# Where a mixture-of-experts kernel issues the casts and subtractions of its second weights, and its gate's steps

## The chip, the cores and the metric

The kernel runs on one core of a Trainium2 chip. The metric is device time in microseconds (us) of one launch. An engine name in a row is the profile's: PE is TensorE's matmul, PEld its weight load, DVE is VectorE, ACT is ScalarE, POOL is GpSimd, and SP issues the DMAs.

## What is computed

The reference is three stages on 1536 tokens of width 512:

```python
x = attention(q, k, v)          # 2 x 8 heads x 768 x 64, 4 sink columns and a window of 128
P = exp(x @ w_gate - max)       # 1536 x 8
for _ in range(8):              # rows, then columns
    P /= P.sum(1, keepdims=True) + 1e-9
    P /= P.sum(0, keepdims=True) + 1e-9
    P *= N / E
for e in range(8):              # every token goes through every expert
    out += P[:, e:e+1] * (relu(x @ w1[e]) @ w2[e])      # 512 -> 1024 -> 512
g = out @ w_in;  g -= tanh(g)                           # 512 -> 2048
return g @ w_out                                        # 2048 -> 512
```

## The kernel before

All products are made of pairs: an operand is split into a high part (`fp32r`, by a cast on ACT) and a low part (the operand less its high part, by a subtraction on DVE or POOL), and three products of parts are summed in PSUM.

**The mixture** (`mixture`, L772) works in 32 half experts, `for u in range(units)` (L859): 16 for the first 768 tokens, 16 for the others. Half expert `u` holds 512 of the 1024 hidden columns in two quartets, a and b, and goes through the list `order` (L856). A step such as `5b` is one of the seven products of a Strassen-like scheme (`product`, L818: six matmuls of 384 columns) for quartet b. Products 1, 6 and 7 write one PSUM bank and their sums are copied out by ACT (`kept`, L812, names `p1`, `u2`, `u3`); products 2, 3 and 7 add such a copy by DVE (`plus`, L816); `put` (L803) then makes the hidden tile by a relu on ACT (L805) and its low part on DVE (L806). Product 6 accumulates on the bank that product 1 left, and 7 on what 6 left, so each waits for the ACT copy before it. The steps g0 to g2, G0 to G2 and A3 to A5 are the second products (`second`, L741: matmuls of 512 columns): g and G take quartets a and b of token tiles 0 to 2, A both of tiles 3 to 5. After G and A, DVE adds the PSUM bank to the sum over experts (L940 in half expert 1, L942, L947), which frees one of the three banks of `ps_g`.

**Weights.** `stage1_next` and `stage2_next` load raw first and second weights by SP's queue. `sum_next` (L549) makes four sums of one raw first tile on POOL (L553); `split1_next` and `split2_next` cast on ACT (L588) and subtract (L591). Of the four casts of first weights per half expert, issued from g2 to G2, three are subtracted on DVE; the fourth is kept in `deferred` and is subtracted on POOL, issued at the start of the next half expert (L868). One second weight is cast and subtracted (on POOL) at that start as well (L870), the other behind product 1a (L901), and there both calls of `sum_next` follow. Every subtraction issues the next load behind it on SP's queue. Each engine works its queue in order, so an instruction issued at a start of a half expert can run earlier on an engine that is ahead of PE.

**Narrow steps.** Up to half expert 28, `some_narrow` (L888) puts ten DVE instructions into each half expert (L686 to L701, eight per piece of 128x512, none in half experts 0, 1 and 15): they round the last layer's weights, one behind 5b, one behind 3a, and one behind each of g0, g1, G0, G1, G2, A3, A4 and A5.

**The gate** (`gates`, L706) is a generator of eleven steps, one taken at each place named in `gate_steps` (L858): the largest logit, its transpose, its broadcast with the first row sums, then eight times a matmul by ones (`pc`, L730) followed by nine DVE instructions (L731 to L735, then L724 to L727) whose result the next `pc` needs. The logits of the second half of the tokens are made in half expert 0 (`gate_logits`, behind 1b to 3a).

**The last layer** (`last_layer`, L976) runs 16 steps of four units (`g1_unit`, `g2_unit`). The first 768 tokens of its input are transposed (`x2_tile`, L969) in half expert 31.

Of the kernel before, what the change touches and what calls it, by code (L numbers as in the profile page):

```python
# [7 lines left out]
F32 = mybir.dt.float32  # L8
# [9 lines left out]
P = 128  # L18
# [5 lines left out]
KD = DM // P  # L24
# [17 lines left out]
class Kernel:  # L42
# [729 lines left out]
    def mixture(self, ctx, gp):  # L772
# [20 lines left out]
        for s in (4, 5, 6):  # L793
            fill(0, s)()
        w2_steps = [step() for _ in range(2) for step in self.split2_next()]
        self.gate_done = False
# [60 lines left out]
        pending, deferred = [], []  # L857
        gate_steps = {0: "g2 G0 G1 A3 A4 A5", 1: "6a 2b 3a g1 G1 A3 A4"}  # L858
        for u in range(units):  # L859
# [6 lines left out]
            held = {}  # L866

            if deferred:  # L868
                deferred.pop()(G)
            if u:  # L870
                w2_steps = [step() for step in self.split2_next()]
            for step in w2_steps:
                step(G)
            if u == 2:
                for i in range(NI):
                    V.tensor_scalar(
                        out=self.acc(0, i), in0=self.acc(0, i), scalar1=prob[:, i, 0:1], scalar2=None, op0=ALU.mult
                    )
            if u == 8:
                for i in range(4):  # L880
                    for k in range(2):
                        self.t_sum(1, i, k, G)
            todo, logits = [], list(range(NI, 2 * NI)) if u == 0 else []
# [10 lines left out]

            for step in order:
                kind, n = step[0], step[1]
                if kind in "1234567":
                    product(qa if n == "a" else qb, int(kind))
                    if logits and step in ("1b", "7a", "2b", "4a", "5b", "3a"):
                        self.gate_logits(logits.pop(0), ps_g, "g")  # L900
                    if step == "1a":  # L901
                        if u:
                            for x in self.split2_next():
                                x()(G)
                        if u < units - 1:
                            self.sum_next()
                            self.sum_next()
                    if step in gate_steps.get(u, "").split():
                        self.gate_bank = lambda shape, name: ps_g.tile(shape, F32, tag="g", name=self.nm(name))
                        next(gates, None)  # L910
                    if step in ("5b", "3a"):
                        some_narrow(1)
                    continue
# [8 lines left out]
                if step == "g2":  # L922
                    todo = self.split1_next() + self.split1_next()
                    if u == units - 1:
                        todo += self.split1_next()
                if todo:
# [23 lines left out]
                if x2s and kind != "g":  # L950
                    self.x2_tile(0, x2s.pop(0), ps_g)
            for second in pending:
# [15 lines left out]

    def x2_tile(self, b, n, pool):  # L969
        pt = pool.tile([P, KD, P], F32, tag="g", name=self.nm("x2"))  # L970
        for d in range(KD):
# [4 lines left out]
    def last_layer(self, ctx, gp):  # L976
# [71 lines left out]

        for _ in range(2):
            for step in self.split2_next():  # L1050
                step()(G)
        for s in range(steps + 1):
            for f in range(4):
                if s < steps:
                    g1_unit(s, f)
                    if (s % 4, f) in ((1, 0), (3, 2)) and s > 1:
                        for step in self.split1_next():
                            step()(G)
                    if (s % 4, f) in ((1, 2), (2, 2)):
                        for step in self.split2_next():  # L1060
                            step()(G)
                elif f == 0:
                    finish_units()
# [39 lines left out]
```

## Time and profile before

| | |
|---|---|
| three runs | 1474.85, 1478.53, 1478.56 us, median 1478.53 |
| the profiled execution | 1477.22 us |
| its span, first to last instruction | 1474.7 us |
| mean granted TensorE clock | 0.995 of full speed |
| PE busy | 1423.6 us (97%), 7367 matmuls |
| DVE busy | 1038.5 us (70%) |
| ACT busy | 704.9 us (48%) |
| POOL busy | 564.5 us (38%) |

Every stretch below is in microseconds from the start of that span. Busy matmul time is modelled and includes overlap, so a stage is better judged by the start of one half expert to the start of the next than by PE's share. A line of the timeline begins with its start and its length, and ends with the engine's idle time before it and what ended it, in brackets.

### The profile page before, as it was taken

The numbers are of one execution on the slowest core, as the hardware profiler recorded it, in microseconds if no ns is written. First come the engines' busy times: TensorE is split into PE (matmuls) and PEld (weight loads), VectorE is DVE, ScalarE is ACT, GpSimd is POOL, SyncE is SP. The second block draws the span as 40 slices with busy tenths as digits, with TensorE's granted clock in tenths as the row PEclk, the third lists the DMA queues.
The fourth block names the chain that finished last, engine by engine and source line by source line (L and its number), as shares of the span: only waits on it lengthen the run. The fifth ranks groups of instructions, "written<-read, shape, count | busy, mean of one in ns | idle before, by whom it ended". The sixth has DMA issues, their size and how long they took to land.

```text
span 1474.7 us, 20203 instructions
## 1 busy us (share of the span) xinstructions
PE 1423.6 (97%) x7367; PEld 1232.7 (84%) x7367; DVE 1038.5 (70%) x1940; ACT 704.9 (48%) x1381; POOL 564.5 (38%) x491
## 2 busy tenths in 40 slices
PE   9998889999999999999999999999999989999998
PEld 6666778888888888887888888888889878888887
DVE  6985676767776677768767677776665577777776
ACT  6986333334333333443333343333334367777764
POOL 1113324434454443334344334434443223444422
PEclk9999999999999999999999999999999999999999
DMA  6332113233332323222333232332221210000001
GB/s 138 83 72 88 58 43 122 79 100 93 100 99 89 113 80 100 85 87 81 106 88 105 80 100 94 100 107 87 92 65 58 83 47 30 29 32 12 1 22 65
DMA packets 141866, 114.76 MB, mean 78 GB/s; under 512 B 43841, under 2 KB 113729, under 8 KB 141761
## 3 DMA queue, kind: packets, MB, share of 16 engines
q1 hardware_dynamic: 141472, 113.42, 25.8%
q8 instruction: 59, 0.97, 0.3%
q14 instruction: 47, 0.38, 0.1%
q10 hardware_dynamic: 288, 0.00, 0.0%
HBM read 101.86 MB, written 11.53 MB: 77 GB/s over the span
## 4 chain that ended last, share of the span: by engine, by line
PE 60%; DVE 23%; ACT 10%; issue 4%; POOL 1%; DMA 1%; SPq 0%; ACTq 0%; POOLq 0%; DVEq 0%
PE pg L746 21%; PE px L831 18%; DVE w1b L591 7%; PE pz L831 7%; PE pa L1006 6%; PE py L831 4%; ACT w1b L588 3%; DVE xa L947 3%; DVE h L806 1%; ACT h L805 1%; ACT an L297 1%; DVE n L697 1%; DVE n L701 1%; DVE pz L816 1%; DVE n L692 1%
## 5 line engine op out<-in xcount | busy, mean ns | idle before, releaser
L746 PE MATMUL pg<-w2b,h 128*128 128x512 f32 x2880 | 705.8, 395 | 28.4 <-DVE xa L947 19.6
L746 PEld LDWEIGHTS pg<-w2b,h 128*128 128x128 f32 x2880 | 534.7, 188 | 160.7 <-DVE xa L947 38.0
L591 POOL TENSOR_TENSOR w2b<-st,w2b 128x1024 fp32r<-128x1024 f32 x72 | 184.8, 2569 | 273.3 <-ACT w2b L588 273.3
L831 PE MATMUL px<-x7c,w1b 128*128 128x384 f32 x1152 | 233.8, 337 | 3.9 <-ACT u L812 2.0
L591 POOL TENSOR_TENSOR w1b<-st,w1b 128x768 fp32r<-128x768 f32 (+1 forms) x36 | 84.8, 2357 | 337.6 <-ACT w1b L588 337.6
L831 PEld LDWEIGHTS px<-x7c,w1b 128*128 128x128 f32 x1152 | 203.6, 189 | 12.4 <-ACT u L812 5.1
L553 POOL TENSOR_TENSOR st<-st 128x256 f32<-128x256 f32 x248 | 194.6, 790 | 14.6
L812 ACT COPY p<-px 128x384 f32<-128x384 f32 x64 | 30.7, 480 | 329.4 <-PE px L831 329.4
L591 DVE TENSOR_TENSOR w1b<-st,w1b 128x1024 fp32r<-128x1024 f32 (+1 forms) x96 | 152.0, 1583 | 12.0 <-ACT w1b L588 12.0
L831 PE MATMUL pz<-x7a,w1b 128*128 128x384 f32 x768 | 148.9, 334 | 0.0
L947 DVE SCALAR_TENSOR_TENSOR xa<-pg,prob,xa 128x512 f32<-128x512 f32 x174 | 128.9, 742 | 21.0 <-PE pg L746 20.9
L1028 POOL TENSOR_TENSOR h<-y,h 128x384 fp32r<-128x384 f32 x63 | 75.5, 1199 | 167.2 <-ACT h L1027 167.2
L831 PEld LDWEIGHTS pz<-x7a,w1b 128*128 128x128 f32 x768 | 134.4, 188 | 0.0
L816 DVE TENSOR_TENSOR u<-u,pz 128x384 f32<-128x384 f32 x64 | 35.5, 554 | 121.4 <-ACT u L812 121.4
L588 ACT CAST w1b<-st 128x1024 fp32r<-128x1024 f32 (+1 forms) x132 | 116.0, 946 | 1.4 <-DMA st<-wf_in 1.4
L812 ACT COPY u<-px 128x384 f32<-128x384 f32 x128 | 61.3, 479 | 99.9 <-PE px L831 99.9
L1017 DVE TENSOR_TENSOR y<-pa,tq 128x384 f32<-128x384 f32 x64 | 35.7, 557 | 65.1 <-ACT th L1015 64.9
L831 PE MATMUL px<-x7a,w1b 128*128 128x384 f32 x384 | 78.8, 340 | 2.4 <-issue 2.4
L831 PE MATMUL py<-x7a,w1b 128*128 128x384 f32 x384 | 76.9, 334 | 0.0
L805 ACT ACTIVATE h<-pz 128x384 fp32r<-128x384 f32 x64 | 31.5, 492 | 93.8 <-DVE pz L816 93.8
L588 ACT CAST w2b<-st 128x1024 fp32r<-128x1024 f32 x72 | 75.4, 1050 | 0.0
L831 PEld LDWEIGHTS px<-x7a,w1b 128*128 128x128 f32 x384 | 69.0, 190 | 5.6 <-issue 3.2
(156 smaller groups left out, 1899.0 us busy)
## 6 DMA issues: line engine op xcount, KB each, us to landing
st<-in_moe_w_dram SPq DMA_DIRECT2D x128, 256.0 KB, 3.2
st<-in_moe_w_dram SPq DMA_DIRECT2D x64, 512.0 KB, 3.9
n<-in_moe_w_in_dram SPq DMA_DIRECT2D x16, 512.0 KB, 3.7
n<-in_moe_w_out_dram SPq DMA_DIRECT2D x16, 512.0 KB, 3.8
wf_in<-n SPq DMA_DIRECT2D x16, 256.0 KB, 2.1
wf_out<-n SPq DMA_DIRECT2D x16, 256.0 KB, 2.1
st<-wf_in SPq DMA_DIRECT2D x8, 512.0 KB, 3.4
st<-wf_out SPq DMA_DIRECT2D x8, 512.0 KB, 3.5
```

Of the source, the lines that this page charges most:

```text
L553: self.nc.gpsimd.tensor_tensor(out=out, in0=a, in1=b, op=op)
L588: self.nc.scalar.copy(out=hi, in_=src)
L591: (engine or self.nc.vector).tensor_tensor(out=lo, in0=src, in1=hi.bitcast(F32), op=ALU.subtract)
L746: self.nc.tensor.matmul(ps, lhsT=self.h[:, f, zh, n * P : (n + 1) * P], rhs=w2[f // 2][:, zw, f % 2, :], start=start and m == 0, stop=stop ...
L805: nc.scalar.activation(out=h[:, f, 0, tok], in_=src, func=AF.Relu)
L812: nc.scalar.copy(out=t, in_=ps)
L816: V.tensor_tensor(out=out, in0=t, in1=ps, op=ALU.add)
L831: nc.tensor.matmul(ps, lhsT=q.w[:, sw, zw, kk * P : (kk + 1) * P], rhs=x[:, zx, kk], start=k in (1, 2, 5) and m == 0, stop=m == 5, skip_gr ...
L947: V.scalar_tensor_tensor(out=a, in0=held[n], scalar=prob[:, b * NI + n, e : e + 1], in1=a, op0=ALU.mult, op1=ALU.add)
L1006: nc.tensor.matmul(ps, lhsT=w[:, zw, kk, f % 2 * P : (f % 2 + 1) * P], rhs=x[zx][:, kk], start=m == 0, stop=m == 3 * KD - 1,)
L1017: V.tensor_tensor(out=y, in0=ps, in1=tq, op=ALU.mult)
L1028: engine.tensor_tensor(out=ht[:, 1], in0=y, in1=ht[:, 0].bitcast(F32), op=ALU.subtract)
```

## The change

Six edits, all in `mixture` and `last_layer`:

1. Nothing is issued at a half expert's start any more. `places` names two products, 1a and 7a (in half expert 0: 5b and 3a). Behind each, one second weight is cast and subtracted; behind the first of them also the deferred subtraction of first weights; then one call of `sum_next`.
2. The eight sums of half expert 8 for the second tokens (`t_sum`) are halved between the two places.
3. Half expert 0 has its own order, in which 5b, 1b and 2b come ahead of 6a, and six steps `L` hold the gate's logits.
4. The gate takes its eleven steps at g1, g2, G0, G2, A3, A4, A5 of half expert 0 and 7a, 6b, g2, G2 of half expert 1 (before: g2, G0, G1, A3, A4, A5, then 6a, 2b, 3a, g1, G1, with two empty ones behind them).
5. The transposes of half expert 31 take banks of `ps_z` instead of `ps_g`.
6. The third split of the last layer's first weights moves from half expert 31 to step 1 of the last layer (subtracted on POOL); its two first splits of second weights move from ahead of the loop to units 2 and 3 of step 0.

```diff
--- before.py
+++ after.py
@@ -792,7 +792,6 @@
 
         for s in (4, 5, 6):
             fill(0, s)()
-        w2_steps = [step() for _ in range(2) for step in self.split2_next()]
         self.gate_done = False
         gates = self.gates(gp)
         narrow = self.narrow_steps()
@@ -855,7 +854,8 @@
         units = 4 * E
         order = "1a 2a 5a 6a 1b 7a 2b 4a 5b 3a 6b g0 7b g1 4b 3b g2 G0 G1 G2 A3 A4 A5".split()
         pending, deferred = [], []
-        gate_steps = {0: "g2 G0 G1 A3 A4 A5", 1: "6a 2b 3a g1 G1 A3 A4"}
+        gate_steps = {0: "g1 g2 G0 G2 A3 A4 A5", 1: "7a 6b g2 G2"}
+        first_order = "1a L 2a 5a 1b 5b 2b 6a L 7a L 4a 3a 6b L 7b L 4b L 3b g0 g1 g2 G0 G1 G2 A3 A4 A5".split()
         for u in range(units):
             b, r = divmod(u, 2 * E)
             e, hf = divmod(r, 2)
@@ -864,22 +864,11 @@
                 q.g, q.w = g, self.w1_view(2 * u + g)
             w2 = [self.w2b[(2 * u + i) % 4] for i in range(2)]
             held = {}
-
-            if deferred:
-                deferred.pop()(G)
-            if u:
-                w2_steps = [step() for step in self.split2_next()]
-            for step in w2_steps:
-                step(G)
             if u == 2:
                 for i in range(NI):
                     V.tensor_scalar(
                         out=self.acc(0, i), in0=self.acc(0, i), scalar1=prob[:, i, 0:1], scalar2=None, op0=ALU.mult
                     )
-            if u == 8:
-                for i in range(4):
-                    for k in range(2):
-                        self.t_sum(1, i, k, G)
             todo, logits = [], list(range(NI, 2 * NI)) if u == 0 else []
             fills = [0, 1, 3, 4, 5, 6, 2] if u == 2 * E - 1 else []
             x2s = list(range(NI)) if u == units - 1 else []
@@ -892,19 +881,27 @@
                 for _ in range(n):
                     next(narrow, None)
 
-            for step in order:
+            places = ("1a", "7a") if u else ("5b", "3a")
+            for step in order if u else first_order:
+                if step == "L":
+                    self.gate_logits(logits.pop(0), ps_g, "g")
+                    continue
                 kind, n = step[0], step[1]
                 if kind in "1234567":
                     product(qa if n == "a" else qb, int(kind))
-                    if logits and step in ("1b", "7a", "2b", "4a", "5b", "3a"):
-                        self.gate_logits(logits.pop(0), ps_g, "g")
-                    if step == "1a":
-                        if u:
-                            for x in self.split2_next():
-                                x()(G)
+
+
+                    if step in places:
+                        for x in self.split2_next():
+                            x()(G)
+                        if deferred:
+                            deferred.pop()(G)
                         if u < units - 1:
                             self.sum_next()
-                            self.sum_next()
+                        if u == 8:
+                            for i in (0, 1) if step == places[0] else (2, 3):
+                                for k in range(2):
+                                    self.t_sum(1, i, k, G)
                     if step in gate_steps.get(u, "").split():
                         self.gate_bank = lambda shape, name: ps_g.tile(shape, F32, tag="g", name=self.nm(name))
                         next(gates, None)
@@ -921,8 +918,6 @@
                 pending = []
                 if step == "g2":
                     todo = self.split1_next() + self.split1_next()
-                    if u == units - 1:
-                        todo += self.split1_next()
                 if todo:
                     (pending if len(todo) > 1 or u == units - 1 else deferred).append(todo.pop(0)())
                 if fills and step != "g0" and step != "g1":
@@ -948,7 +943,7 @@
                             out=a, in0=held[n], scalar=prob[:, b * NI + n, e : e + 1], in1=a, op0=ALU.mult, op1=ALU.add
                         )
                 if x2s and kind != "g":
-                    self.x2_tile(0, x2s.pop(0), ps_g)
+                    self.x2_tile(0, x2s.pop(0), ps_z, "z")
             for second in pending:
                 second()
             pending = []
@@ -966,8 +961,8 @@
             both = [buf[:, (2 * s % 4 + z) * n : (2 * s % 4 + z + 1) * n] for z in range(2)]
         return [t.rearrange("p (k n) -> p k n", k=KD) for t in both]
 
-    def x2_tile(self, b, n, pool):
-        pt = pool.tile([P, KD, P], F32, tag="g", name=self.nm("x2"))
+    def x2_tile(self, b, n, pool, tag="g"):
+        pt = pool.tile([P, KD, P], F32, tag=tag, name=self.nm("x2"))
         for d in range(KD):
             self.nc.tensor.transpose(pt[:, d], self.acc(b, n)[:, d * P : (d + 1) * P], self.ident)
         x, tok = self.x2(b, n // 3), slice(n % 3 * P, (n % 3 + 1) * P)
@@ -1046,17 +1041,14 @@
                     r0 = (b * NI + n) * P
                     nc.sync.dma_start(out=self.out[r0 : r0 + P, c0:c1], in_=a[:, c0:c1])
 
-        for _ in range(2):
-            for step in self.split2_next():
-                step()(G)
         for s in range(steps + 1):
             for f in range(4):
                 if s < steps:
                     g1_unit(s, f)
-                    if (s % 4, f) in ((1, 0), (3, 2)) and s > 1:
+                    if (s % 4, f) in ((1, 0), (3, 2)):
                         for step in self.split1_next():
                             step()(G)
-                    if (s % 4, f) in ((1, 2), (2, 2)):
+                    if (s % 4, f) in ((1, 2), (2, 2)) or s == 0 and f >= 2:
                         for step in self.split2_next():
                             step()(G)
                 elif f == 0:
```

## Rows read from the trace of the kernel before

**Rows 1.** What PE waited for, whole span: us in total, times, longest.

```profile
PE pg L746 <- DVE xa L947: 19.6, 32, 1.5
PE pc L730 <- DVE prob L727: 5.6, 3, 2.1
PE pg L746 <- ACT h L1027: 3.5, 2, 1.9
PE pg L746 <- DVE xa L940: 2.4, 1, 2.4
...
PE x L972 <- DVE xa L947: 1.3, 1, 1.3
```

**Rows 2.** Timeline of PE: product 1a of half experts 2, 15, 17, 29, 30.

```profile
214.53 1.23 PE L831 MATMUL px<-x7a,w1b 128*128 128x384 f32 x6
...
636.30 0.87 PE L831 MATMUL px<-x7a,w1b 128*128 128x384 f32 x4
...
702.81 1.23 PE L831 MATMUL px<-x7a,w1b 128*128 128x384 f32 x6
...
1090.53 1.23 PE L831 MATMUL px<-x7a,w1b 128*128 128x384 f32 x6
...
1121.54 1.23 PE L831 MATMUL px<-x7a,w1b 128*128 128x384 f32 x6
```

**Rows 3.** Timeline of POOL, DVE and PE, second products of half expert 6.

```profile
366.27 2.33 POOL L591 TENSOR_TENSOR w1b<-st,w1b 128x768 fp32r<-128x768 f32 x1 [10.27 <-ACT w1b L588]
368.56 2.84 POOL L591 TENSOR_TENSOR w2b<-st,w2b 128x1024 fp32r<-128x1024 f32 x1
...
366.81 2.34 DVE L697 SCALAR_TENSOR_TENSOR n<-n,n 128x512 f32<-128x512 uint16 x1
...
373.81 3.06 PE L746 MATMUL pg<-w2b,h 128*128 128x512 f32 x12 [0.89 <-DVE xa L947]
```

**Rows 4.** Two narrow steps by line: duration in ns, min/median/max.

```profile
L697 DVE SCALAR_TENSOR_TENSOR n<-n,n x32: 673/683/2341, 237.4 to 1074.7; 128x512 f32<-128x512 uint16 x32
...
L690 DVE TENSOR_SCALAR n<-n x32: 409/420/577, 228.1 to 1069.1; 128x512 int32<-128x512 int32 x32
```

**Rows 5.** Timeline by engine, products of half expert 6; first row from half expert 15.

```profile
660.59 1.85 POOL L591 TENSOR_TENSOR w1b<-st,w1b 128x768 fp32r<-128x768 f32 x1 [12.52 <-ACT w1b L588]
...
346.93 2.40 POOL L591 TENSOR_TENSOR w2b<-st,w2b 128x1024 fp32r<-128x1024 f32 x1 [7.78 <-ACT w2b L588]
349.29 6.71 POOL L553 TENSOR_TENSOR st<-st 128x256 f32<-128x256 f32 x8
...
352.28 0.60 DVE L806 SCALAR_TENSOR_TENSOR h<-u,h 128x384 fp32r<-128x384 f32 x1 [0.59 <-ACT h L805]
...
354.86 0.55 DVE L686 TENSOR_SCALAR n<-n 128x512 int32<-128x512 int32 x1
...
355.91 0.49 ACT L805 ACTIVATE h<-pz 128x384 fp32r<-128x384 f32 x1 [1.64 <-DVE pz L816]
356.30 0.47 ACT L812 COPY u<-px 128x384 f32<-128x384 f32 x1
...
357.01 1.22 PE L831 MATMUL px<-x7c,w1b 128*128 128x384 f32 x6
```

**Rows 6.** Half expert 0: ACT; PE; stretch (PE, PEld, DVE, ACT, POOL, PEclk).

```profile
132.77 1.99 ACT L588 CAST w2b<-st 128x1024 fp32r<-128x1024 f32 x2
...
135.28 1.99 PE L831 MATMUL px<-x7c,w1b 128*128 128x384 f32 x6 [1.87 <-ACT p L812]
...
135.30:139.00 3.70, 3.70 (x13) 3.70 (x14) 1.04 (x2) 0.97 (x2) 3.70 (x3) 0.54 0.45 123
```

**Rows 7.** Half expert 1: two gate instructions on DVE, then a stretch as above.

```profile
173.24 2.32 DVE L725 TENSOR_SCALAR rs<-rs 128x12 f32<-128x12 f32 x1
...
181.04 0.75 DVE L735 TENSOR_TENSOR prob<-prob,cs 128x96 f32<-128x96 f32 x1
...
189.00:194.00 5.00, 5.00 (x19) 4.44 (x19) 3.14 (x12) 0.97 (x2) 0.00 (x0) 0.66 0.00 0
```

## The prediction, made before the change was run

> **What bounds the kernel now.** Begin with what PE waited for over the whole span [rows 1]. PE is nearly always busy, so only its waits can be given back: 32 times it waited for the DVE addition L947 (19.6 us), three times for the gate (5.6), once for L940 (2.4). Then read what a half expert takes, from product 1a to the next 1a [rows 2]: 13 of them from 214.53 to 636.30 are 32.44 us each, 12 from 702.81 to 1090.53 are 32.31, and the one from 1090.53 to 1121.54, when the narrow steps are used up, is 31.01. So a half expert with narrow steps (32.39 on average) loses about 1.38 us; half experts 15 and 16, in between, are taken apart below.
>
> Why it loses them stands in the timeline of its second products [rows 3]. POOL subtracts a first weight (366.27, 2.33 us) and right behind it a second one (368.56). The narrow step L697 begins inside the first, at 366.81, and takes 2.34 us, to 369.15, 0.55 behind the end of POOL's instruction. By itself it takes 0.68 [rows 4]. So a DVE instruction whose operands all lie in SBUF is held until the POOL instruction that began before it ends. The additions L947 queue behind it on DVE, and A5 waits 0.89 us for its bank.
>
> **Second products (edits 1).** The two POOL subtractions that ran there ran ahead of PE; the change issues them behind 1a of the next half expert, whose copy and cast they must wait for. The hold of 1.66 us (2.34 less 0.68) exceeds the wait of 0.89, and nothing else in this stretch uses POOL. I take all of the 1.38 us as given back. What is late next is DVE's own work; between 1090.53 and 1121.54 it delays nothing.
>
> **The products (edit 1): the price.** POOL's work now lies in a row behind 1a. I walk it in half expert 6 [rows 5], which began at 344.16. The first subtraction begins at 346.93 as before, the next instruction at 349.29. The deferred one takes 1.85 where DVE doesn't disturb it: to 351.1. Four sums at 6.71/8 = 0.84 each: to 354.5. Then comes the subtraction of the second weight of 7a, whose cast (about 1 us behind the relu of 7a) is ready before: from 354.5 to about 356.9. The narrow step of 5b is issued at 354.86 on DVE, about 0.4 us behind the start of that subtraction. So it is held to 356.9 and done by some 357.2 instead of 355.40: 1.8 us late.
>
> Queued behind it on DVE is the addition of product 3a; behind that on ACT the relu (355.91); behind the relu the copy `u2` of 6b (356.30 to 356.77); and for that copy waits 7b on PE, which began at 357.01. The slack is 0.24 us, so 7b waits about 1.5, and 1.6 with the first loads that no longer hide. The narrow step of 3a then meets sums of under 1 us, and POOL is done before g2. All four kinds of step that come behind 5b (L686, L690, L694, L699) have their operands in SBUF. A half expert then takes 31.01 + 1.6 = 32.6 against 32.39 on average: +0.2 us, times 26 is **+5.7 us**. The bounds of the wait: 1.1 if the subtraction begins 0.4 earlier; 2.1 if it begins just ahead of the narrow step; 0 if it begins behind it.
>
> The Trainium skill ("SBUF — State Buffer", Who interferes with whom) states the hold as an exclusive lock, and that issue order, not the shape of the operation, decides who blocks. Rows 3 agree: 2.34 us for the one that came second. By that rule the sum below holds with POOL's subtraction first at 5b, and with the narrow step first it would be rival 1's 1432 us.
>
> **Half expert 0 (edits 1 and 3).** Two casts (1.99 us) stood on ACT ahead of the copy for which 6a waited 1.87 us [rows 6]. Now three more products come ahead of 6a, and the casts come later: -2.0 with its restart. From 135.3 to 139.0 the granted clock was 0.54, most of it at the lower level (1.2 GHz), behind that wait: 3.7 x 0.46 = 1.7 us, of which I take 1.5. Against that, the cast behind 3a stands ahead of the copy of 6b: relu, cast and copy end some 1.3 us after 7b could begin, though a logit step covers a part. Sum **-2.2** (bounds -4 and 0).
>
> **Half expert 1 (edit 4).** Before: gate waits of 5.6, the wait for L940 of 2.4 [rows 1], and 5.0 us at a clock of 0.66, that is 1.7 us lost [rows 7]: 9.7. These waits came from holds as well: L725 took 2.32 under a subtraction, and L735 0.75 under a sum. After: the step behind A5 is done before POOL begins. The one at 7a puts nine instructions on DVE ahead of the addition of 2b, five of them SBUF only; sums hold three or four by up to 0.7, and the subtraction holds one for 2.3, so the chain takes some 5.5 us instead of 2.3. The matmul behind 6b then waits 2.5 us, g0 0.5, 7b 1.1: 4.1, and the rest fits. POOL is idle from g2 on, so the 2.4 goes too: 9.7 to 4.3, **-5.4** (bounds -9 and -1).
>
> **Half experts 15 and 16.** They took 702.81 - 636.30 = 66.5 us. Without POOL's holds the refill of the inputs of the second tokens on DVE ends before 1a of 16; 31.0 + 32.6 = 63.6: **-2.9** (bounds -4 and 0). Moving the sums of half expert 8 spreads POOL's work, which ends before the cast that needs it by little: 0.
>
> **The last layer (edits 5 and 6).** The transposes in half expert 31 no longer wait for a bank of `ps_g` [rows 1]: -1.3, -2 with the restarts. The cast and subtraction of first weights (about 1.0 and 2.4) and the two of second weights now lie inside steps 0 and 1, where PE already waits for ACT (3.5 [rows 1]). They delay ACT by a cast and hold DVE by up to 1.7 each: +3. Sum **+1** (bounds -3 and +4). SP's queue: each load goes out behind its subtraction, now up to 10 us later, but is needed a half expert (32 us) later; the narrow loads behind them have as long. These cost nothing as long as the first-weight load issued behind the deferred subtraction lands before POOL's second four sums.
>
> **Sum.** -2.2 - 5.4 - 2.9 + 5.7 + 1 = -3.8 on the profiled execution's 1477.2: **1473.4 us**. That execution lies 1.3 below the median of the three runs (1478.53), and runs differ by 3.7. About 0.3% (4.4 us) is what can be told from no change; 1473.4 lies just outside it.
>
> **Rivals.**
> 1. *The narrow step of 5b comes first.* If POOL is 0.4 us later than walked (a sum lengthened by DVE's L806, as 352.28 with 0.60 shows, could give 0.3), the step slips in at the end of a sum and nothing holds it. Then the 1.38 us stays gained: -2.2 - 5.4 - 2.9 - 26 x 1.38 + 1 = -45.4, **1432 us**. For it: the margin is small. Against it: a held L806 also delays DVE's own queue by 0.2, and the walk leaves POOL early, not late.
> 2. *The hold falls at its longest* (slower). If the subtraction begins just ahead of the narrow step, at 354.8, 7b waits 2.1 us, 33.2 us per half expert: +0.8 x 26 = +21, sum +11.5, **1489 us**. It decides from a start of about 354.6 on, where the wait at 7b is over 1.6. For it: POOL's chain has five links that can each be late. Against it: only a window of 0.2 us leads here.
> 3. *The opening gives nothing*: the gate's chain is held as long as before, and the lower clock stays. Then halves 0 and 1 are worth 0 to -1: +3, **1480 us**.
>
> **How the numbers follow.** Forecast 0.60, with its own range 1464 to 1484; rival 1 0.22, rival 2 0.12, rival 3 0.06. The range reaches from rival 1's time to near rival 2's: 1431 to 1487. Faster by over 0.3% (under 1474.1): rival 1 and half of the forecast, 0.53. Slower (over 1483): rival 2 and a little of the forecast, 0.16. The same: 0.31.
>
> **What would show it.** Right: PE's waits for L947 nearly gone; a new wait of product 7b for the ACT copy of L812, about 1.5 us in each of 26 half experts; the narrow step at 5b as long as 2.3 us; POOL idle from g2 to A5; gate waits of 2 to 4 us in half expert 1. Wrong: no such wait at 7b (then rival 1), half experts of 33 us (rival 2), or waits for L947 that stay without POOL beside them.

## The result, and the profile after

The changed kernel takes 1488.91 us (median of five runs, 1487.05 to 1491.26), the kernel before 1478.53: a ratio of 1.008, 95% interval 1.0061 to 1.01. It is slower by 0.8%. (One slow run of five of the kernel before, at 1592.86 us, is left out of the ratio.) The forecast was a small gain, 1473.4 us, and the range ended at 1487. The profiled execution took 1488.91 us with a span of 1487.0, against a span of 1474.7 before: 12.3 us to be found.

What PE waited for, over the whole span (us in total, times, longest), to be held against [rows 1]:

```profile
PE px L830 <- ACT u L811: 42.5, 27, 6.9
...
PE pc L730 <- DVE prob L727: 2.5, 1, 2.5
PE pg L746 <- DVE xa L942: 2.1, 1, 2.1
...
PE pa L1001 <- DVE x7a L58: 1.4, 1, 1.4
```

(Some lines have new numbers: the product is L830, the copy to SBUF L811, the addition L815, the relu L804, its low part L805, the scaled addition L942, formerly L947.) The 19.6 us behind the scaled addition are gone but for one wait of 2.1, and 42.5 us of waits for the copy have come in, 27 times, once with 6.9. Two of them (1.5 us) lie in half experts 0 and 1, the other 25 are product 7b's in half experts 2 to 28, without 8 and 15.

Then the starts of product 1a, in the timeline of PE (half experts 0, 1, 2, 3, then 8, 9, then 15, 17, 29, 31), to be held against [rows 2]:

```profile
130.23 0.66 PE L830 MATMUL px<-x7a,w1b 128*128 128x384 f32 x1 [2.71 <-issue]
173.47 0.42 PE L830 MATMUL px<-x7a,w1b 128*128 128x384 f32 x1
210.01 0.51 PE L830 MATMUL px<-x7a,w1b 128*128 128x384 f32 x2
250.42 0.51 PE L830 MATMUL px<-x7a,w1b 128*128 128x384 f32 x2
...
413.85 0.51 PE L830 MATMUL px<-x7a,w1b 128*128 128x384 f32 x2
449.13 0.51 PE L830 MATMUL px<-x7a,w1b 128*128 128x384 f32 x2
...
645.60 0.51 PE L830 MATMUL px<-x7a,w1b 128*128 128x384 f32 x2
709.23 0.51 PE L830 MATMUL px<-x7a,w1b 128*128 128x384 f32 x2
...
1101.85 0.51 PE L830 MATMUL px<-x7a,w1b 128*128 128x384 f32 x2
...
1163.87 0.51 PE L830 MATMUL px<-x7a,w1b 128*128 128x384 f32 x2
```

And before, where [rows 2] doesn't show them: half experts 0, 3, 8, 9 and 31.

```profile
130.02 1.30 PE L831 MATMUL px<-x7a,w1b 128*128 128x384 f32 x6 [2.39 <-issue]
...
247.31 0.51 PE L831 MATMUL px<-x7a,w1b 128*128 128x384 f32 x2
...
409.97 0.51 PE L831 MATMUL px<-x7a,w1b 128*128 128x384 f32 x2
...
442.05 0.51 PE L831 MATMUL px<-x7a,w1b 128*128 128x384 f32 x2
...
1152.55 1.23 PE L831 MATMUL px<-x7a,w1b 128*128 128x384 f32 x6
```

The difference between two starts is a half expert (half expert 1 began at 171.46 before). The forecast's +5.7 for 26 half experts is 0.22 for each. Against the same differences before, the 12.3 us come apart like this:

| stretch | before | after | forecast | measured |
|---|---|---|---|---|
| half expert 0 | 41.44 | 43.24 | -2.2 | +1.8 |
| half expert 1 | 43.07 | 36.54 | -5.4 | -6.5 |
| half expert 2 | 32.78 | 40.41 | +0.2 | +7.6 |
| 3 to 7 and 9 to 14 | 356.9 | 359.9 | +2.4 | +3.0 |
| half expert 8 | 32.08 | 35.28 | +0.2 | +3.2 |
| 15 and 16 | 66.51 | 63.63 | -2.9 | -2.9 |
| 17 to 28 | 387.7 | 392.6 | +2.6 | +4.9 |
| 31 to the end | 322.15 | 323.1 | +1 | +1.0 |

With 0.2 ahead of half expert 0 they add up to 12.3 (29 and 30 take 62.02 us in both). Three rows are wrong by 3 us or more: half experts 0, 2 and 8.

The repeating loss is the one that was walked. Half expert 6 in the timelines of POOL, DVE, ACT and PE:

```profile
358.86 2.40 POOL L591 TENSOR_TENSOR w2b<-st,w2b 128x1024 fp32r<-128x1024 f32 x1
...
359.45 2.08 DVE L686 TENSOR_SCALAR n<-n 128x512 int32<-128x512 int32 x1
361.46 0.55 DVE L815 TENSOR_TENSOR pz<-u,pz 128x384 f32<-128x384 f32 x1
...
362.04 0.49 ACT L804 ACTIVATE h<-pz 128x384 fp32r<-128x384 f32 x1 [3.18 <-DVE pz L815]
362.43 0.47 ACT L811 COPY u<-px 128x384 f32<-128x384 f32 x1
...
362.96 1.31 PE L830 MATMUL px<-x7c,w1b 128*128 128x384 f32 x6 [1.35 <-ACT u L811]
```

The subtraction of the second weight has run 0.59 us when the narrow step begins; the step takes 2.08 instead of 0.55 [rows 5] and ends 0.27 behind it. Addition, relu and copy follow one behind the other, and 7b waits 1.35 us.

Half expert 2 has its own cause. SP's queue before (first fence); SP's queue and POOL after (second); the waits of DVE and PE after, and a stretch behind them (third; us, busy PE, PEld, DVE, ACT, POOL; then the granted clock):

```profile
220.07 0.37 SPq L537 DMA_DIRECT2D st<-in_moe_w_dram  x1
220.49 0.93 SPq L669 DMA_DIRECT2D n<-in_moe_w_in_dram  x2
```

```profile
223.07 0.37 SPq L537 DMA_DIRECT2D st<-in_moe_w_dram  x1
223.49 0.94 SPq L669 DMA_DIRECT2D n<-in_moe_w_in_dram  x2
...
220.63 2.41 POOL L591 TENSOR_TENSOR w2b<-st,w2b 128x1024 fp32r<-128x1024 f32 x1
```

```profile
228.04 0.43 DVE L686 TENSOR_SCALAR n<-n 128x512 int32<-128x512 int32 x1 [6.72 <-DMA n<-in_moe_w_in_dram]
228.38 0.56 DVE L815 TENSOR_TENSOR pz<-u,pz 128x384 f32<-128x384 f32 x1
...
229.88 2.29 PE L830 MATMUL px<-x7c,w1b 128*128 128x384 f32 x6 [6.86 <-ACT u L811]
...
231.00:234.50 3.50, 3.50 (x10) 2.96 (x10) 1.14 (x3) 1.00 (x2) 0.00 (x0) 0.50 0.00 0
```

The very first narrow piece is loaded only when the first narrow step is issued, at 5b of half expert 2, and its loads L669 stand on SP's queue behind the load L537 of the next second weight, which waits for POOL's subtraction (to 223.04 after) to free its buffer. Counted from 1a, they went out 220.49 - 214.53 = 6.0 us in before and 223.49 - 210.01 = 13.5 after: 7.5 us later, where half expert 2 lost 7.6. DVE, in order, stood 6.72 us at that step, and the addition of 3a behind it. That 7.5 and 7.6 are so near is chance. PE waited 6.9 us for the copy, and behind that wait it ran at the lower of its clock levels (0.50, 1.2 GHz) to 234.5, an estimated 2.3 us more: with the 31.0 us of a half expert without waits that makes 40.2 of the 40.41. The 32.78 us of before held 1.8 us of other losses.

In half expert 8 the four `t_sum` pairs at 7a make POOL's row longer. Its end, and DVE in the second products:

```profile
435.28 2.96 POOL L644 TENSOR_TENSOR tsum<-xa 128x384 f32<-128x384 f32 x2
438.20 2.85 POOL L644 TENSOR_TENSOR tsum<-xa,tsum 128x384 f32<-128x384 f32 x2
...
435.52 1.86 DVE L591 TENSOR_TENSOR w1b<-st,w1b 128x1024 fp32r<-128x1024 f32 x1 [0.38 <-ACT w1b L588]
437.30 1.22 DVE L686 TENSOR_SCALAR n<-n 128x512 int32<-128x512 int32 x1
438.44 0.74 DVE L942 SCALAR_TENSOR_TENSOR xa<-pg,prob,xa 128x512 f32<-128x512 f32 x1
```

DVE's own subtraction and the narrow step behind it are held, the scaled addition comes late, and PE waits 2.1 us for it (the first view). Then the clock is at 0.50 from 440 to 443, an estimated 1.5 us. At 5b there is no hold in this half expert: with the other four sums ahead of it, POOL's second-weight subtraction begins at 428.66, 3.9 us behind the narrow step.

### The profile page after: what moved, and what is told of

It reads as the page before. It is cut to its first block, busy times and chain, and to the rows that moved or that the text cites. A ratio compares the mean times of both kernels' runs of the same rounds, so it can differ in the third digit from the quotient of the medians.

```text
span 1487.0 us, 20185 instructions
## 1 busy us (share of the span) xinstructions
PE 1420.0 (95%) x7367; PEld 1241.1 (83%) x7367; DVE 1010.4 (68%) x1939; ACT 704.1 (47%) x1381; POOL 544.4 (37%) x492
## 4 chain that ended last, share of the span: by engine, by line
PE 68%; DVE 12%; ACT 8%; issue 6%; POOL 3%; DMA 1%; SPq 0%; POOLq 0%; DVEq 0%; ACTq 0%
PE pg L746 37%; PE px L830 14%; PE pa L1001 6%; PE pz L830 5%; DVE h L805 3%; PE py L830 3%; ACT h L804 2%; ACT u L811 2%; ACT an L297 1%; POOL h L1023 1%; POOL st L553 1%; DVE n L690 1%; DVE n L686 1%; DVE n L699 1%; DVE u L815 1%
## 5 line engine op out<-in xcount | busy, mean ns | idle before, releaser
L746 PE MATMUL pg<-w2b,h 128*128 128x512 f32 x2880 | 693.6, 394 | 8.1 <-POOL w2b L591 3.5
L591 POOL TENSOR_TENSOR w2b<-st,w2b 128x1024 fp32r<-128x1024 f32 x72 | 173.6, 2411 | 618.2 <-ACT w2b L588 618.2
L830 PE MATMUL px<-x7c,w1b 128*128 128x384 f32 x1152 | 235.4, 339 | 42.5 <-ACT u L811 42.5
L830 PEld LDWEIGHTS px<-x7c,w1b 128*128 128x128 f32 x1152 | 202.4, 189 | 57.5 <-ACT u L811 54.3
L553 POOL TENSOR_TENSOR st<-st 128x256 f32<-128x256 f32 x248 | 201.6, 813 | 14.6
L811 ACT COPY p<-px 128x384 f32<-128x384 f32 x64 | 30.7, 479 | 324.9 <-PE px L830 324.9
L942 DVE SCALAR_TENSOR_TENSOR xa<-pg,prob,xa 128x512 f32<-128x512 f32 x174 | 129.8, 747 | 68.4 <-PE pg L746 68.4
L830 PE MATMUL pz<-x7a,w1b 128*128 128x384 f32 x768 | 149.7, 336 | 0.0
L830 PEld LDWEIGHTS pz<-x7a,w1b 128*128 128x128 f32 x768 | 135.3, 189 | 0.0
L591 DVE TENSOR_TENSOR w1b<-st,w1b 128x1024 fp32r<-128x1024 f32 (+1 forms) x95 | 108.2, 1140 | 11.3 <-ACT w1b L588 11.3
L811 ACT COPY u<-px 128x384 f32<-128x384 f32 x128 | 61.2, 478 | 96.1 <-PE px L830 96.1
L815 DVE TENSOR_TENSOR u<-u,pz 128x384 f32<-128x384 f32 x64 | 35.2, 551 | 104.4 <-ACT u L811 104.4
L804 ACT ACTIVATE h<-pz 128x384 fp32r<-128x384 f32 x64 | 31.4, 491 | 135.6 <-DVE pz L815 135.6
L830 PE MATMUL px<-x7a,w1b 128*128 128x384 f32 x384 | 79.5, 342 | 2.7 <-issue 2.7
L830 PE MATMUL py<-x7a,w1b 128*128 128x384 f32 x384 | 78.0, 338 | 0.0
L830 PEld LDWEIGHTS px<-x7a,w1b 128*128 128x128 f32 x384 | 69.8, 192 | 5.8 <-issue 3.5
L1001 PE MATMUL pa<-x7a,w1b 128*128 128x384 f32 x384 | 73.2, 343 | 1.4 <-DVE x7a L58 1.4
```

The lines of the kernel that those rows point to most:

```text
L553: self.nc.gpsimd.tensor_tensor(out=out, in0=a, in1=b, op=op)
L591: (engine or self.nc.vector).tensor_tensor(out=lo, in0=src, in1=hi.bitcast(F32), op=ALU.subtract)
L746: self.nc.tensor.matmul(ps, lhsT=self.h[:, f, zh, n * P : (n + 1) * P], rhs=w2[f // 2][:, zw, f % 2, :], start=start and m == 0, stop=stop ...
L804: nc.scalar.activation(out=h[:, f, 0, tok], in_=src, func=AF.Relu)
L811: nc.scalar.copy(out=t, in_=ps)
L815: V.tensor_tensor(out=out, in0=t, in1=ps, op=ALU.add)
```

## The experiments

In these runs the kernel before took 1477.3 to 1477.8 us (medians), and the ratios are to it. The theory: every narrow step at 5b is held by POOL's second-weight subtraction, which began first; on top of that the first narrow load is late, and half expert 8's sums hold DVE. The main rival: these waits only cover a loss that stays when they go, or any step of DVE among the first products costs as much.

**The narrow step of 5b issued behind g2.**

```diff
-                    if step in ("5b", "3a"):
+                    if step == "3a":
...
-                if step != "g2":
-                    some_narrow(1)
+                some_narrow(1)
```

> The changed kernel with one edit: the narrow step behind 5b is issued behind g2. Theory (the wait of 7b comes from that step, held on DVE by the second subtraction of second weights): the waits of 7b for the copy on ACT go in all 26 half experts with narrow steps, 31.0 to 31.1 us each instead of 32.6, which is -42 us; half expert 2 loses most of its 40.4 us too, as its first narrow step no longer stands ahead of the addition of 3a (33 us). Time 1489 - 42 - 7 = 1440 us. Rival (DVE is simply full, and a step more among the second products brings the waits for L942 back): half experts stay at 32.3 us or more, 1480 us.

Measured: 1439.06 us (1438.48 to 1441.78), ratio 0.9742 (0.9724 to 0.9761), as the theory had it. Half experts 3 to 28 take 31.01 us each but for half expert 8 (33.77). What PE waited for:

```profile
PE pz L830 <- DVE u L815: 3.2, 1, 3.2
...
PE px L830 <- ACT u L811: 1.5, 2, 0.9
```

Of the 42.5 us behind the copy L811 only the 1.5 in half experts 0 and 1 are left. The spans differ by 47.1 us (1487.0 and 1439.9): 42.3 of them from the start of half expert 3 to that of 29, 4.3 in half expert 2. What is left there is the late load, now met at 3a: 36.12 us.

**The first narrow loads issued in half expert 1.**

```diff
         load(0)
+        load(1)
+        yield
         for i in range(32):
-            load(i + 1)
+            if i:
+                load(i + 1)
...
+            if u == 1:
+                next(narrow)
```

> The changed kernel with one edit: the first two raw pieces of the narrow steps are loaded at the start of half expert 1 instead of at the first narrow step in half expert 2. Theory (that load stood on SP's queue behind a load that waits for GpSimd, and DVE waited for it 6.7 us): half expert 2 takes 32.6 us instead of 40.4, with a wait of 7b of 1.3 to 1.6 and no lower clock behind it; all others as they were. Time 1489 - 7.8 = 1481 us. Rival (the six multiplications of the sums by the gate, at the start of half expert 2, put DVE behind): half expert 2 stays at 40 us and the time at 1489.

Measured: 1480.07 us (1478.28 to 1481.4), ratio 1.0019 (1.0008 to 1.0029). Half expert 2 takes 33.01, and the longest wait for the copy (L814 in this kernel) is 1.7 in place of 6.9:

```profile
PE px L833 <- ACT u L814: 36.9, 27, 1.7
```

So the load's place on SP's queue, with the lower clock that followed it, was 7.4 of the 7.6 us that half expert 2 lost; the granted clock of the whole half expert is 1.00 here and 0.92 in the changed kernel.

**POOL's four sums ahead of the second subtraction at 7a.**

```diff
                     if step in places:
+                        if u < units - 1 and step == places[1]:
+                            self.sum_next()
                         for x in self.split2_next():
...
-                        if u < units - 1:
+                        if u < units - 1 and step == places[0]:
                             self.sum_next()
```

> The changed kernel with one edit: behind 7a the four sums are issued ahead of the cast and subtraction of the second weight. Theory (the length of the instruction that holds the narrow step of 5b sets the wait: 2.4 us for a subtraction, 0.8 for a sum): 7b waits 0 to 0.3 us, half experts with narrow steps take 31.0 to 31.4 us, 1489 - 26 x 1.4 = 1452 us. If the sums must wait for their load and start late, DVE finds GpSimd idle at 5b and the wait goes as well. Rival (any work of GpSimd at that place, or DVE's own queue, makes 7b wait): 32.6 us and 1489.

Measured: 1464.74 us (1463.25 to 1469.07), ratio 0.9922 (0.9896 to 0.9949); the half experts take 31.2 to 32.6. The hold at 5b goes, but the subtraction is only moved on, and sometimes meets a later DVE instruction; half expert 2 gets worse (44.13), since the load that waits for the subtraction waits longer (the narrow loads go out 16.9 us behind 1a, not 13.5). The direction was right, the size two thirds (24 us of 37).

```profile
PE px L830 <- ACT u L811: 15.4, 16, 10.4
```

**The sums of half expert 8 spread**, one behind 1a of each of half experts 4 to 11.

```diff
-                        if u == 8:
-                            for i in (0, 1) if step == places[0] else (2, 3):
-                                for k in range(2):
-                                    self.t_sum(1, i, k, G)
+                        if 4 <= u < 12 and step == places[0]:
+                            self.t_sum(1, *divmod(u - 4, 2), G)
```

> The changed kernel with only the t_sums of half expert 8 spread, one behind 1a of each of half experts 4 to 11. Theory (the four at 7a hold DVE into the second products): half expert 8 falls from 35.3 to 32.65, half experts 4 to 11 stay at 32.65 or lose up to 0.3 each by a later POOL: 1486 to 1488.5. Rival (the refill of the second sums has its price wherever it lies): no change, 1488.9.

Measured: 1474.70 us (one run), 14 us less than the changed kernel; neither theory had that. Half expert 8 takes 31.52, and the seven others that got one more POOL instruction take 31.26 to 31.54 instead of 32.63 to 32.92. Half expert 6, POOL and DVE:

```profile
356.67 1.02 POOL L644 TENSOR_TENSOR xa<-xa 128x384 f32<-128x384 f32 x1
357.64 2.59 POOL L591 TENSOR_TENSOR w2b<-st,w2b 128x1024 fp32r<-128x1024 f32 x1
...
357.26 0.70 DVE L686 TENSOR_SCALAR n<-n 128x512 int32<-128x512 int32 x1
```

One more instruction of 1.02 us delays the subtraction past the narrow step, which now begins 0.38 us ahead of it, near the end of that instruction, and takes 0.70. That is the mechanism of rival 1, come about by more work on POOL.

**The narrow step of 5b issued behind 4a** (`("5b", "3a")` becomes `("4a", "3a")`).

> The changed kernel with the narrow step of 5b issued behind 4a, one product earlier. Theory (only the order against POOL's subtraction of the second weight matters: beside the single sums a step is held by less than 0.84 us): half experts 3 to 7 fall from 32.65 to 31.0 to 31.5 us, half expert 2 keeps its wait for the load, 1448 to 1458 us. Rival (any narrow step among the first products delays the chain to 7b): half experts stay at 32 us or more, 1475 us or more.

Measured: 1488.14 us (1486.82 to 1491.85), ratio 1.0067 (1.0042 to 1.0092), the half experts 32.63 as after. A miss of the experiment, not of the rival: 5b issues nothing on DVE, so DVE's order is the same as in the changed kernel, and the step runs behind the same low part.

**The narrow step of 5b issued behind 7a** (`("7a", "3a")`).

> The changed kernel with the narrow step of 5b issued behind 7a. Behind 4a it kept its place on DVE, since 5b gives DVE nothing to do; behind 7a it stands ahead of two additions and two low parts of products 2b and 4a, so it begins among POOL's single sums, about 1.5 us before the subtraction of the second weight. Theory (the order against that subtraction decides): half experts 3 to 7 take 31.0 to 31.5 us in place of 32.65, half expert 2 stays at 40 us or more, 1449 to 1457 us. Rival (any step among the first products delays the chain to 7b): the step delays the addition of 2b and what follows, half experts of 31.8 us or more, 1467 us or more.

Measured: 1459.40 us (1459.05 to 1460.18), ratio 0.9877 (0.986 to 0.9893). Half experts 31.5 to 31.8, half expert 2 41.45. DVE, POOL and PE in half expert 6:

```profile
354.97 0.96 DVE L686 TENSOR_SCALAR n<-n 128x512 int32<-128x512 int32 x1
...
356.49 2.40 POOL L591 TENSOR_TENSOR w2b<-st,w2b 128x1024 fp32r<-128x1024 f32 x1
...
359.39 1.33 PE L830 MATMUL px<-x7c,w1b 128*128 128x384 f32 x6 [0.23 <-ACT u L811]
```

The step runs 1.5 us ahead of the subtraction and is held only by a sum (0.96). 1.1 of the 1.64 us are back without taking any DVE work out of the first products. The time lies 2 us above the theory's range and 8 below the rival's. 7b still waits 0.23 us for its copy, and a half expert is 0.5 longer than with the step behind g2, so a step among the first products, here held only by a sum, still has a price, though a smaller one.

**The old order in half expert 0** (`first_order` and its logit steps as before, the casts behind 5b and 3a).

> The changed kernel with one edit: half expert 0 in the order of before, with its logits behind the same products as before (the casts stay behind 5b and 3a). Theory A (the lower clock from 130 to 139 us in half expert 0 is not the order's doing: it began ahead of the first product): the granted clock of 130 to 139 differs from run to run with either order, and where it is low half expert 0 takes 42 to 43 us with the old order too; where it is full, about 39. Theory B (the new order with a logit step behind product 1a keeps the clock low): clock full from 130 to 135 as before, half expert 0 of 38 to 40 us, time 1489 - 4 = 1485.

Measured: 1485.36 us (1484.42 to 1485.83), ratio 1.0058 (1.0039 to 1.0077); half expert 0 takes 39.88: theory B's numbers, but without its full clock, which is 0.68 from 130 to 135.3 (1.00 in the first profile of before). **And the kernel before once more**, without any edit:

> The kernel before once more, for a second profile of its opening. Theory (the granted clock in half expert 0 differs from run to run): the stretch from 130 to 139.3 us shows a mean clock that differs from the 1.00 and 0.57 of the first profile by 0.1 or more, and half expert 0 differs from 41.44 us by 0.5 or more. Rival (the order of the products sets the clock): the same clock to 0.05 and half expert 0 within 0.3 of 41.44.

Measured: 1477.38 us (one run), half expert 0 at 40.38. The stretch from 127 to 139.3 in before, in its second profile, in the changed kernel, in the kernel with the step at 4a (the same order on every engine), and in the old order (us, busy PE, PEld, DVE, ACT, POOL; then the granted clock):

```profile
127.00:139.30 12.30, 8.04 (x36) 7.15 (x34) 3.82 (x5) 6.18 (x10) 5.40 (x3) 0.86 0.70 214
```

```profile
127.00:139.30 12.30, 9.77 (x43) 9.17 (x42) 3.98 (x6) 6.61 (x10) 4.92 (x3) 0.72 0.67 196
```

```profile
127.00:139.30 12.30, 9.59 (x33) 9.10 (x32) 3.93 (x6) 3.75 (x6) 0.00 (x0) 0.58 0.58 175
```

```profile
127.00:139.30 12.30, 9.71 (x40) 9.21 (x39) 3.89 (x6) 4.38 (x8) 0.00 (x0) 0.72 0.57 175
139.30:163.00 23.70, 23.04 (x114) 21.60 (x114) 7.96 (x18) 8.62 (x15) 10.72 (x10) 0.78 0.15 45
```

```profile
127.00:139.30 12.30, 9.69 (x51) 9.26 (x49) 3.98 (x6) 4.95 (x9) 0.00 (x0) 0.86 0.58 175
```

Length times (1 - clock) estimates what the lower level cost: 1.7 and 3.4 us in the two profiles of before, 5.2 after, 3.4 + 5.2 = 8.6 with the step at 4a (half expert 0: 47.02), 1.7 in the old order. So the same program meets a different clock from run to run. Less that, half expert 0 takes 43.24 - 5.2 = 38.0 in the new order and 39.88 - 1.7 = 38.2 in the old one, but the same working gives 39.7 and 37.0 for the two profiles of before. It is too rough for a difference of this size, probably since a slower PE also hides waits: the second profile of before, at 0.50 from 130 to 135.3, shows no wait of 6a for its copy, 1.87 us in the first [rows 6].

Profiles with the same clock in both stretches compare better. At 0.86 and 1.00 half expert 0 takes 40.68 us in the new order (the kernel with the sums ahead), 39.88 and 39.79 in the old one with the casts moved (this one and the last but one below); at 0.72 and 1.00 it takes 42.27 and 42.26 (early loads; all three repairs) against 41.12 (the last one below). So the new order is about 1 us longer by itself. 0.7 of it is a wait of 7b for its copy, which the three kernels in the old order don't have.

**The gate's steps back at their old places.**

```diff
-        gate_steps = {0: "g1 g2 G0 G2 A3 A4 A5", 1: "7a 6b g2 G2"}
+        gate_steps = {0: "g2 G0 G1 A3 A4 A5", 1: "6a 2b 3a g1 G1 A3 A4"}
```

> The changed kernel with only the places of the gate's steps as before (half expert 0: g2 G0 G1 A3 A4 A5; half expert 1: 6a 2b 3a g1 G1 A3 A4). Theory (the gain of 6.5 us in half expert 1 comes from the moved gate steps, together with POOL's subtractions leaving the second products): half expert 1 back to 40 us or more, with waits for the gate's L727 of 5 us or more in place of 2.5: 1492 us or more. Rival (POOL's move alone gave it, the places matter little): half expert 1 at 36 to 38 us, 1488 to 1490.

Measured: 1491.83 us (one run); half expert 1 takes 39.38, with gate waits of 3.5. Both numbers lie between the two expectations. Half expert 1 in before, after and this kernel:

```profile
171.46:214.53 43.07, 35.09 (x170) 30.40 (x168) 32.91 (x72) 13.35 (x22) 14.74 (x12) 0.96 0.21 59
```

```profile
173.47:210.01 36.54, 33.04 (x168) 28.88 (x166) 25.59 (x63) 12.48 (x21) 12.53 (x11) 1.00 0.18 58
```

```profile
174.81:214.19 39.38, 35.90 (x169) 32.15 (x168) 28.20 (x72) 12.59 (x21) 12.42 (x11) 0.91 0.18 54
```

PE was not busy for 43.07 - 35.09 = 8.0 us before, 3.5 after and 3.5 here, so in these profiles POOL's leaving gave the waits back, and the places none of them (a slower PE may hide some here). The prediction's walk through the moved step got its wait right (2.5), but the old places have as much in all. The 2.8 us by which this run is longer are PE at the lower clock (39.38 x 0.09 = 3.5). The old places aren't needed for that clock: two kernels with the new ones (early loads, and the last one below) have 0.91 in half expert 1 as well, and take 38.73 and 38.92 there.

**All three repairs together** (the step behind g2, the early loads, the spread sums), first in the new order of half expert 0, then in the old.

> The changed kernel with the narrow step of 5b issued behind g2, the first two narrow loads issued in half expert 1, and the eight t_sums of half expert 8 issued singly behind 1a of half experts 4 to 11. Theory (each of the three places loses its own time, independently of the others): from the 1439.1 us of the run with only the step moved, half expert 2 falls from 36.1 to about 31.3 us, half expert 8 from 33.8 to 31.0: 1431.5 us. Rival (the loss of half expert 2 comes from the clock, and the sums of half expert 8 are covered): half experts 2 and 8 stay as they are, 1438 to 1440.

> As the combined kernel, but half expert 0 in the order of before, with the logit steps at their old places; the casts of the second weights stay behind 5b and 3a. Theory (the new order gives nothing, and the clock there is low for some microseconds with either order): 0 to 3.5 us faster than the combined kernel with the new order, half expert 0 at 40 to 42 us. Rival (the new order removes a wait of 1.9 us for 6a and keeps the clock up): 2 us slower than it.

Measured: 1432.60 us (1431.86 to 1438.08), ratio 0.9706 (0.9689 to 0.9722), and 1431.84 us (1431.7 to 1433.1), ratio 0.9694 (0.9681 to 0.9708). Half expert 2 takes 31.01 in both, half expert 8 31.20 and 31.18: the repairs add up. The two orders can't be told apart by these times. (Without the repairs all four runs in the old order, 1484.4 to 1485.8, lie below all five in the new one, 1487.1 to 1491.3.)

**As the last one, with edit 6 undone** (the last layer's weights prepared as before; the transposes keep their bank of `ps_z`).

```diff
+                    if u == units - 1:
+                        todo += self.split1_next()
...
+        for _ in range(2):
+            for step in self.split2_next():
+                step()(G)
...
-                    if (s % 4, f) in ((1, 0), (3, 2)):
+                    if (s % 4, f) in ((1, 0), (3, 2)) and s > 1:
...
-                    if (s % 4, f) in ((1, 2), (2, 2)) or s == 0 and f >= 2:
+                    if (s % 4, f) in ((1, 2), (2, 2)):
```

> As the combined kernel with the old opening, and also the last layer's weights prepared as before (third first-weight part at g2 of half expert 31, two second-weight parts ahead of the loop, none in steps 0 and 1), while the transposes keep their bank from ps_z. Theory (the last layer's +1 was -1.3 to -2 from the transposes and +3 from casts and subtractions in steps 0 and 1): the stretch from the start of half expert 31 to the end is 2 to 3 us shorter, 1429 to 1430 us. Rival (the two edits need each other: the parts at the end of half expert 31 hold DVE there and take back what the transposes gave): no shorter, 1431 to 1433.

Measured: 1430.74 us (1427.48 to 1432.58), ratio 0.9673 (0.965 to 0.9696). Half expert 31 starts at 1106.69 in the kernel with the old opening (span 1430.0) and at 1110.51 in this one (span 1430.6):

```profile
1106.69 0.51 PE L833 MATMUL px<-x7a,w1b 128*128 128x384 f32 x2
```

```profile
1110.51 0.51 PE L833 MATMUL px<-x7a,w1b 128*128 128x384 f32 x2
```

From there to the end it is 323.3 against 320.1 us. But in the eleven kernels that have edit 6 this stretch takes 320.8 to 323.3, so that the edit's cost lies between 0.7 and 3.2: the theory's direction held, its 2 to 3 us aren't settled. In the run's time the gain is covered by half experts 0 and 1 (80.0 us here, 76.4 in the kernel with the old opening). By its median this is the fastest kernel, 3.3% below before and 3.9% below the changed one, but it isn't told apart from the one ahead of it.

## Why the prediction was wrong

**Right: the second products and the price.** The waits for the scaled addition went, 7b waits 1.35 (1.62 to 1.64 in every fourth half expert, where the narrow step is L699) instead of the walked 1.5 to 1.6, and half experts take 32.65 where 32.6 was forecast. Half experts 15 and 16 take 63.63 (63.6), half expert 1 gave 6.5 us (5.4), by POOL's leaving rather than by the gate's new places, as far as one run with the old places shows. The repeating term is 7.9 us over half experts 3 to 14 without 8 and 17 to 28, where the forecast gives 5.0 to these 23; most of the difference lies in the six of them that take 32.9. (Its count of 26 held half expert 16, which had its own term: 0.2 us. The mean of the 25 half experts is 32.38, not 32.39, and the waits listed for half expert 1 come to 4.1, where the sum goes on with 4.3.)

**Right by luck: the last layer.** +1.0 was measured where +1 was forecast, but the kernels that share this code spread over 2.5 us, and the median of the eleven is 321.8, a little below the 322.15 of before. The transposes' wait of 1.3 us, which was to be won, came back as 1.4 us of the last layer's first product, which waits for the low part of a transposed tile (the last line of the first view).

**Rival 1 was a real neighbour, rival 2 only met the number.** The runs with spread sums and with the step behind 7a show that 1 us of POOL's time, or a step 1.5 us ahead of the subtraction, gives back 1.1 to 1.4 us in each half expert. The margin that was walked as 0.4 us measured 0.59. The 1489 us of rival 2 is not its mechanism: 7b never waited 2.1 us outside half expert 2.

The Trainium skill ("SBUF — State Buffer", Who interferes with whom) describes an exclusive lock, which whoever issues first holds for the whole instruction while the other is blocked. The runs agree from both sides: 2.08 us for the step that began 0.59 behind the subtraction, 0.70 for the one 0.38 ahead of it.

**Wrong, the step that failed most: "These cost nothing".** The prediction let SP's later loads pass, since "the narrow loads behind them have as long", a half expert. That holds for every piece but the first. Piece 0 is loaded when it is first wanted, with no lead at all. So the 7.5 us by which it went out later behind POOL's subtraction became 6.7 us of DVE's and 6.9 of PE's waiting, and the lower clock behind that wait. Half expert 2 took 7.6 us more, and moving that load alone gave 7.4 back. A cost in one half expert out of 32 was looked for with the rule of the other 31.

**Wrong: "Moving the sums of half expert 8 spreads POOL's work ... 0".** Only the cast that needs the sums was checked, not who is held at POOL's new end. The walk had POOL "done before g2"; in half expert 8 it ran to 441.05, far into the second products. +3.2.

**Wrong: half expert 0's -2.2.** The clock's term failed: of 1.7 us at the lower level 1.5 were to be won back, and 3.5 more were lost. One profile of before was taken as the rule, where the second one lost 3.4 us to the clock and doesn't even have the wait of 6a. Reordering and moving the casts together were to give -2.0 + 1.3; against the old order with the casts moved, where 6a doesn't wait either, the new order costs about 1 us. The sum of the three misses, 7.4 + 3.0 + 4.0 = 14.4, and the 2.9 by which the repeating term was short, less 1.1 from half expert 1, make 16.2, which is to 0.1 the distance from -3.8 to +12.3.

What stays open: the new order met a lower clock more often. Half expert 0 took 40.7 to 47.0 us in nine kernels with it, 39.8 to 41.1 in three with the old order and the casts moved; by the working above the lower level cost 1.7 to 8.6 us in the nine, 1.7 to 3.4 in the three and in the two profiles of before. But runs of one instruction order differ by 3.4 us, so the order isn't shown to be the cause.

## What to carry to other kernels

When a wait on one queue moves, look at the first and the last user of everything behind it: a steady loop can hide a late load by its lead, while its first turn may have none. Where two engines exclude each other, ask which instruction begins first before you ask how long it is, and a margin of 0.4 us repeated in 25 places is worth finding out by moving the instruction before the change is built. An instruction moved past products that issue nothing on its engine hasn't moved.

## What the runs showed of the hardware

The hold works both ways: the subtraction that began inside a narrow step took 2.59 us instead of 2.40. A single-operand step (L686) was held as a two-operand one was (L699: 2.35 us).

The granted clock at the opening differed between runs of the same instruction order by an estimated 3.4 us of lost time (5.2 and 8.6). The Trainium skill ("TensorE: Matmul & The Clock Gate", Part 1) says that the window which the gate goes by runs freely and does not reset when a kernel starts, so that the point of the change shifts. The profiles here agree in that the same order met different clocks.
